# Four small edits at the edges of a two-cache decode attention: a projection moved inside the first tile, the last weight load in four pieces, a later x load, two loads issued ahead of the block

## The chip, the cores and the metric

The kernel runs on one core of a Trainium2 chip. The metric is the device time of one execution in microseconds (us). Beside it each run lists the *span*, the time from the first to the last instruction of the core; here the time is 1.7 us longer than the span in most runs, and that difference becomes a finding further down.

## The reference, cut to what matters

Two independent attention layers, "cache A" and "cache B", each decode one token for 8 batch entries and 32 heads. Every operand is bf16.

```python
B, Sq, D = 8, 1, 1024
H, Sk, Dh = 32, 4096, 128
q = (x @ wq).reshape(B, Sq, H, Dh).transpose(0, 2, 1, 3)
scores = einsum("bhqd,bhkd->bhqk", q, k_cache) * (Dh ** -0.5)
o = einsum("bhqk,bhkd->bhqd", softmax(scores), v_cache)
out = o.transpose(0, 2, 1, 3).reshape(B, Sq, H * Dh) @ wo
# the same for A and for B; the two outputs are concatenated
```

Each cache has 268 MB of k and as much of v, all read once. That makes some 1.1 GB for little arithmetic.

## The kernel before

The work is cut into 64 tiles (2 caches, 8 batch entries, 4 groups of 8 heads). A tile has one k load and one v load of 8.4 MB each, 64 KB per partition. Three ring slots hold them. Each engine runs its own list of operations in order: PE the matrix products, DVE the vector work, ACT copies and the exponential, and SP issues loads. A load is issued by SP when the slot's last user on PE is done.

The order of loads, and the rule by which a load may be issued:

```python
plan = [("wq", 0, 1), ("k", 0, 0), ("wq", 1, 2)]          # (what, which, ring slot)
for n in range(NQ - 1):
    plan.append(("k", n + 1, (n + 1) % 2))
    plan.append(("v", n, 2))
plan += [("v", NQ - 1, NQ % 2), ("wo", 0, 2), ("wo", 1, (NQ - 1) % 2)]
tenant = [None, None, ("x", 0)]
# ... load_tiles(): the next load of the plan depends on opUse of the slot's former tenant:
#     wq -> the q products; k -> the last chunk's sums on PE; v -> the second half of the P.V products
```

So slot 2 has, in turn, x, wq of B, v of tile 0, v of tile 1, and so on. The v load of tile 1 has to wait for the P·V products of tile 0, and those run in chunks 2 and 3 of tile 1.

A tile's k is handled in four chunks (`NR` is 4). DVE multiplies a chunk by q, folds it once, PE sums further, DVE reduces. With cuts:

```python
for n in range(NQ):
    for r in range(NR):
        s = n * NR + r
        make_mul(s)                     # DVE, L330, 4.4 us; waits for k
        if s >= LAG: make_red(s - LAG)  # DVE, L353
        # ... softmax shift and exp of tile n - 1 at r == 0
        fold = make_fold(s)             # DVE, L335, 2.3 us
        # ... make_pm(n - 1) at r == 0: the weights for P.V of tile n - 1
        if n == 0 and r == 1:
            for c in range(1, NC):
                make_q(c)               # PE: x @ wq of B, waits for wq of B; ACT copies the result
                make_qT(c)              # PE transposes, DVE copies four times (L305)
        if r == 2 and n >= 1: make_pv(n - 1, 0, RG // 2)
        if r == 3 and n >= 1: make_pv(n - 1, RG // 2, RG); make_acc(n - 1)
        # ...
        make_eacc(s, fold)              # PE, L345
        load_tiles()
```

The last weight load, wo of B, is cut by heads so that the products can follow the pieces:

```python
wo_cuts = ((0, H - 8), (H - 8, H - 2), (H - 2, H))       # 24, 6 and 2 heads
# ... in load_tiles: one dma per cut, each with its own semaphore ("w", i)
# ... in make_proj, for the last cache:
for i, (r0, r1) in enumerate(wo_cuts):
    def emit(e, r0=r0, r1=r1):
        for r in range(r0, r1):
            for q in range(nt):                           # nt is 4: four products per head
                x = e.matmul(proj[32 * q:32 * q + B, 0:dt], on_sb[:, c, r, :], w[:, col:col + dt], ...)
    opProj[c] = add("pe", emit, [opNorm[c], opT[("wo", c, i)], c_proj, opEv.get(c - 1)])
```

Two more parts that the change touches: x is loaded through ACT's queue with no dependency, and everything, the first loads too, is issued inside one `nc.Block()`.

Of the kernel before, what the change touches and what calls it, by code (L numbers as in the profile page):

```python
# [31 lines left out]
class _Program:  # L32
# [11 lines left out]
    def add(self, eng, emit, deps=(), dma_key=None, moves=False):  # L44
        op = _Op(eng, emit, list(deps), dma_key, moves)
        if dma_key is not None:
            self.counts[dma_key] = self.counts.get(dma_key, 0) + 16
            op.token = (dma_key, self.counts[dma_key])
        for d in op.deps:
            if not (d.eng == "pe" and eng == "pe"):  # L50
                d.sig = True
        self.ops[eng].append(op)
        return op
# [29 lines left out]
            waited.update(left)  # L83
        return out, known

    def run(self, engname, eng, sems, loop=None):
        ops = self.ops[engname]
        waits, known = self._waits(engname)

        def emit(op, at=lambda base, step: base):  # L90
            ins = op.emit(eng, at) if op.moves else op.emit(eng)
            if op.dma_key is not None:
                ins.then_inc(sems[op.dma_key], 16)
            elif op.sig:
                ins.then_inc(sems[op.eng], 1)

        def straight(lo, hi):
            for op, left in zip(ops[lo:hi], waits[lo:hi]):
                for key, val in left.items():
                    eng.wait_ge(sems[key], val)  # L100
                emit(op)

        if loop is None:
            straight(0, len(ops))
            return
        first, per, rounds = loop
        at = [self.marks[first + per * i][engname] for i in range(rounds + 1)]
        size = at[1] - at[0]
        assert all(y - x == size for x, y in zip(at, at[1:]))
        body, step = [], {}  # L110
        for j in range(size):
            rows = [waits[lo + j] for lo in at[:-1]]
            row = {}
            for key in rows[1]:
                grow = rows[2][key] - rows[1][key]
                row[key] = rows[1][key] - grow
                assert step.setdefault(key, grow) == grow

                assert rows[0].get(key) == row[key] or key not in rows[0] and row[key] <= known[at[0] + j].get(key, 0), (engname, j, key)
            for i, r in enumerate(rows):  # L120
                assert ops[at[i] + j].sig == ops[at[0] + j].sig
                assert set(r) <= set(row) and (i == 0 or r == {key: val + i * step[key] for key, val in row.items()}), (engname, j, i)
            body.append(row)
        straight(0, at[0])
        with eng.Fori(0, rounds) as i:
            grown = {x: eng.snap(i * x) for x in sorted(set(step.values()))}
            moved = {}

            def place(base, x):
                if x not in moved:  # L130
                    moved[x] = eng.snap(i * (x * per))
                return moved[x] + base
            for j in range(size):
                for key, val in body[j].items():
                    eng.wait_ge(sems[key], grown[step[key]] + val)  # L135
                emit(ops[at[0] + j], place)
        straight(at[-1], len(ops))


def _build_kernel(nc, caches, out):  # L140
    B, Sq, D = caches[0][0].shape
    _, H, Sk, Dh = caches[0][1].shape
    NC = len(caches)
# [7 lines left out]
    NR = T // CT  # L151
# [8 lines left out]

    es = ExitStack()
    with es:
        block = es.enter_context(nc.Block())
        sb = lambda name, shape, dt: es.enter_context(nc.sbuf_tensor(name, shape, dt))
        ps = lambda name, n=512: es.enter_context(nc.psum_tensor(name, [128, n], FP32))

# [29 lines left out]
        q_ps = [o_ps, pv_ps]  # L196
        misc_bf16 = misc.bitcast(BF16)

        wo_cuts = ((0, H - 8), (H - 8, H - 2), (H - 2, H))
        sems = {e: es.enter_context(nc.semaphore(f"c_{e}")) for e in ENGINES[1:]}  # L200
        for name, n in (("t", 3), ("w", len(wo_cuts)), ("x", 1), ("out", 1)):
            for i in range(n):
# [2 lines left out]
        P = _Program()  # L205
        add = P.add

        def dma(out_ap, in_ap, key, deps, eng="sp"):
            return add(eng, lambda e: e.dma_start(out_ap, in_ap), deps, dma_key=key)
# [16 lines left out]
        c_oh = add("dve", lambda e: e.tensor_copy(own_h[:], own), [c_own])  # L226
# [100 lines left out]
        def make_mul(s):  # L327
            n = s // NR
            v = chunk(s).rearrange("p (t d) -> p t d", d=Dh)
            opMul[s] = add("dve", lambda e: e.tensor_tensor(  # L330
                v, v, qbc[:, n % 2, :].unsqueeze(1).to_broadcast([128, CT, Dh]), ALU.mult), [opT[("k", n)], opQbc[n]])

        def make_fold(s):
            v = chunk(s).rearrange("p (t d) -> p t d", d=Dh)
            return add("dve", lambda e: e.tensor_tensor(v[:, :, 0:64], v[:, :, 0:64], v[:, :, 64:128], ALU.add), [opMul[s]])  # L335
# [15 lines left out]
        def make_red(s):  # L351
            n, r = divmod(s, NR)
            opRed[s] = add("dve", lambda e: e.tensor_reduce(  # L353
                s_sb[:, n % 2, r * CT:(r + 1) * CT], red_ps[s % 2][:, :].rearrange("p (t w) -> p t w", w=16), AX.X, ALU.add),
                [opEacc[s], _at(opExp, n - 2)])


        def make_shift(n):
            m = add("dve", lambda e: e.tensor_reduce(rmax[:], s_sb[:, n % 2, :], AX.X, ALU.max), [opRed[NR * n + NR - 1]])  # L359
            t = add("dve", lambda e: e.tensor_scalar(rtmp[:].rearrange("p (i w) -> p i w", i=2),  # L360
                                                     half[:].unsqueeze(2).to_broadcast([128, 2, 16]), rmax[:, 0:1], scale,
                                                     ALU.add, ALU.mult), [m, c_half])
            opNgm[n] = add("dve", lambda e: e.tensor_reduce(ngm[:, n % 2:n % 2 + 1], rtmp[:], AX.X, ALU.max, negate=True,  # L363
                                                            apply_transpose=True), [t, _at(opExp, n - 2)])
            opExp[n] = add("act", lambda e, at: e.activation(pe[:], s_sb[:, n % 2, :], ACTF.Exp, bias=ngm[:, n % 2:n % 2 + 1], scale=scale,  # L365
                                                             accum_out=rsum[:, bass.ds(at(n, 1), 1)]),
                           [opNgm[n], _at(opPM, n - 1)], moves=True)

        def make_pm(n):
            opPM[n] = add("dve", lambda e: e.tensor_tensor(PM[:], pe[:].unsqueeze(2).to_broadcast([128, T, HQ]),  # L370
                                                           own_h[:].unsqueeze(1).to_broadcast([128, T, HQ]), ALU.mult),
                          [opExp[n], c_oh, _at(opPV, n - 1), opQT["last"] if n == 0 else None])
# [16 lines left out]
        def make_acc(n):  # L389
            opAcc[n] = add("act", lambda e: e.activation(accS[:], pv_ps[:], ACTF.Copy), [opPV[n], _at(opExt, n - 1)])  # L390
# [51 lines left out]


        x_sb = ring[0:B, 2, 0:NC * D].rearrange("p (c d) -> p c d", c=NC)
        op_x = [dma(x_sb[:, c, :], caches[c][0].rearrange("b s d -> b (s d)"), ("x", 0), [], "act") for c in range(NC)]

        def emit_xT(e):
            for c in range(NC):
# [14 lines left out]
        for n in range(NQ):  # L463
            P.mark(n)
            for r in range(NR):
                s = n * NR + r
                make_mul(s)
                if s >= LAG:
                    make_red(s - LAG)
                if r == LAG - 1 and n >= 1:  # L470
                    make_shift(n - 1)
                fold = make_fold(s)
                if r == LAG - 1 and n >= 1:
                    make_pm(n - 1)
                if n == 0 and r == 1:
                    for c in range(1, NC):
                        make_q(c)
                        make_qT(c)
                if r == 2 and n >= 1:
                    make_pv(n - 1, 0, RG // 2)  # L480
                if r == 3 and n >= 1:
                    make_pv(n - 1, RG // 2, RG)
                    make_acc(n - 1)
                if r == 2 and n + 1 < NQ:
                    make_stage(n + 1)
                    make_qbc(n + 1)
                make_eacc(s, fold)
                load_tiles()
                if r == 3 and n >= 1:
                    make_ext(n - 1)  # L490
        P.mark(NQ)
        n = NQ - 1
# [15 lines left out]
            o.token = (("x", 0), 16 * NC)  # L508
        loops = {"pe": (1, 2, (NQ - 2) // 2), "dve": (3, 2, (NQ - 4) // 2), "act": (3, HB, (NQ - 4) // HB)}

        @block.sync
        def _(eng):
            P.run("sp", eng, sems)
            eng.wait_ge(sems[("out", 0)], counts[("out", 0)])

        @block.tensor
# [49 lines left out]
```

## Time and profile before

| | before |
|---|---|
| time, median of 5 runs (range) | 2566.68 us (2566.35 to 2567.43) |
| span of the profiled run | 2565.3 us |
| bytes moved, mean rate | 1107.51 MB, 432 GB/s |
| DVE busy, PE busy | 85%, 44% |

The first view is the profile page. In the line of the tenths, each digit is one of 40 equal slices of the span, and 9 is 90% or more.

```profile
DVE  2898898898898898898888888988988988988983
...
DMA  9999999999999999999999999999999999999998
...
DMA packets 19435, 1107.51 MB, mean 432 GB/s; under 512 B 2209, under 2 KB 2257, under 8 KB 2401
...
q1 hardware_dynamic: 19344, 1107.32, 99.8%
```

The loads fill 99.8% of the time of all 16 DMA engines. No other engine can be the limit, and no edit that leaves the bytes alone can do more than fill the few gaps. To find them one has to look finer than a slice of 64 us. The next view is the timeline of DVE in before, from the start of the multiplies; the columns are start, duration, engine, line, operation, output<-input, and in brackets how long the engine had been idle and what released it.

```profile
55.39 2.28 DVE L335 TENSOR_TENSOR ring<-ring 128x4096 bf16<-128x4096 bf16 x1
69.66 0.43 DVE L305 COPY qT<-misc 128x64 bf16<-128x64 bf16 x1 [11.99 <-PE misc L301]
...
72.67 4.54 DVE L330 TENSOR_TENSOR ring<-ring,qbc 128x8192 bf16<-128x8192 bf16 x1
...
88.12 4.42 DVE L330 TENSOR_TENSOR ring<-ring,qbc 128x8192 bf16<-128x8192 bf16 x1
```

In the middle of tile 0, after chunk 1, DVE stands still for 12 us because the copies of q of cache B come next in its list. The k of tile 0 lies there ready. The last line is chunk 0 of tile 1: it starts at 88.12. The same delay shows on the queue that issues the loads (timeline of SP in before):

```profile
67.90 0.33 SPq L209 DMA_DIRECT2D ring<-in_A_v_cache_dram  x1
91.89 0.33 SPq L209 DMA_DIRECT2D ring<-in_A_k_cache_dram  x1
118.20 0.33 SPq L209 DMA_DIRECT2D ring<-in_A_v_cache_dram  x1
125.70 0.33 SPq L209 DMA_DIRECT2D ring<-in_A_k_cache_dram  x1
```

The third line is the v load of tile 1. The packet records of the trace (start, duration and size of each DMA packet) show what it runs into. The load ahead of it, k of tile 2, ends like this on the 16 engines, and the next load starts like this:

```
before, 64 KB packets near 119 us
ends of the old load:   118.50 118.55 118.55 118.57 118.69 118.71 118.74 118.80 118.80 118.80 118.81 118.83 118.92 118.92 120.14 120.24
starts of the new load: 119.16 119.17 119.17 119.18 119.18 119.26 119.27 119.28 119.30 119.34 119.36 119.36 119.45 119.68 120.24 121.84
duration of the new load's first 14 packets: 2.70 to 3.64 us;  of a packet in the stream: 2.42 us
```

About 1 us passes from the issue to the first packet, the old load is out by then, and the first packets after a pause are slower. The means of the two rows differ by 0.6 us. That is the one hole in the whole record, after the start and before the end, in which the 16 engines stood idle for more than 0.3 us on average.

The last part is the end. The chain that ended last, in before, from the last products of the softmax on (start, duration, what):

```profile
2521.87 34.98 DMA ring<-in_B_wo_dram
2556.84 0.14 issue
2556.98 5.66 PE proj L433 x96
2562.64 0.02 issue
2562.66 0.42 DVE orow L438
```

And the table of stretches for the same kernel; the columns after the stretch are its length, the busy time of PE, PEld, DVE, ACT and POOL with the number of instructions, the granted TensorE clock (1.00 is full), the DMA share and GB/s:

```profile
2557.00:2559.00 2.00, 2.00 (x40) 1.36 (x44) 0.00 (x0) 0.00 (x0) 0.00 (x0) 0.50 0.79 326
2559.00:2561.00 2.00, 2.00 (x47) 1.28 (x39) 0.00 (x0) 0.00 (x0) 0.00 (x0) 0.50 0.22 88
2561.00:2563.00 2.00, 1.61 (x56) 1.15 (x48) 0.34 (x1) 0.00 (x0) 0.00 (x0) 0.99 0.03 10
```

PE starts when the piece of 24 heads has landed, and works without a pause for 5.66 us, most of it at half clock, while the loads thin out and end at 2561.30.

### The profile page before, as it was taken

Reading aid. Unit: us, or ns where it says so; the run is one execution under the profiler, and the core shown is the slowest. Engines: PE = TensorE matmul, PEld = TensorE weight load, DVE = VectorE, ACT = ScalarE, POOL = GpSimd, SP = SyncE. Lnnn points to the kernel's source line nnn. Section 1 sums busy time; section 2 is a strip of 40 time slices with the busy share of each in tenths; the row PEclk is TensorE's granted clock in tenths of the full one; section 3 lists DMA queues with packets and bytes.
Section 4 is the critical chain, followed back from the end, with each engine's and each line's share of the span. In section 5 each row is a group of like instructions: output and inputs, shape, how many; then the busy total and the mean of one; then the engine's idle time right before and its main releaser. Section 6 shows DMA issues by size and latency. Waiting matters only on the chain.

```text
span 2565.3 us, 18707 instructions
## 1 busy us (share of the span) xinstructions
PE 1125.5 (44%) x7648; PEld 395.3 (15%) x7648; DVE 2172.4 (85%) x1043; ACT 130.0 (5%) x401; POOL 2.6 (0%) x14
## 2 busy tenths in 40 slices
PE   2543443444444444444444434444444434434435
PEld 0111111111111111111111111111111111111112
DVE  2898898898898898898888888988988988988983
ACT  1100000000000000000000000000000000000000
POOL 0000000000000000000000000000000000000000
PEclk7666667676766767767766767667766757667677
DMA  9999999999999999999999999999999999999998
GB/s 425 425 425 441 433 433 433 433 435 431 435 431 435 431 435 432 435 431 435 432 435 431 435 431 436 430 436 430 437 429 437 429 437 430 436 431 435 431 436 381
DMA packets 19435, 1107.51 MB, mean 432 GB/s; under 512 B 2209, under 2 KB 2257, under 8 KB 2401
## 3 DMA queue, kind: packets, MB, share of 16 engines
q1 hardware_dynamic: 19344, 1107.32, 99.8%
q8 instruction: 7, 0.11, 0.0%
q10 hardware_dynamic: 80, 0.05, 0.0%
q14 instruction: 4, 0.02, 0.0%
HBM read 1107.33 MB, written 0.03 MB: 432 GB/s over the span
## 4 chain that ended last, share of the span: by engine, by line
DMA 51%; DVE 28%; issue 16%; PE 5%; another core or an unknown queue 0%; ACT 0%; DVEq 0%; SPq 0%
DMA ring<-in_B_k_cache_dram 25%; DMA ring<-in_A_k_cache_dram 25%; DVE ring L330 10%; DVE ring L335 10%; PE red L345 4%; DVE s_sb L353 4%; DVE PM L370 3%; DMA ring<-in_B_wo_dram 1%; DVE rmax L359 1%; DVE rtmp L360 0%; PE proj L433 0%; ACT PM L291 0%; PE o L285 0%; DVEq L135 0%
## 5 line engine op out<-in xcount | busy, mean ns | idle before, releaser
L345 PE MATMUL red<-ring,ident 128*128 128x512 bf16 x2048 | 785.6, 553 | 1380.5 <-DVE ring L335 1380.5
L330 DVE TENSOR_TENSOR ring<-ring,qbc 128x8192 bf16<-128x8192 bf16 x256 | 1131.1, 4418 | 303.4 <-DMA ring<-in_B_k_cache_dram 153.3
L335 DVE TENSOR_TENSOR ring<-ring 128x4096 bf16<-128x4096 bf16 x256 | 581.4, 2271 | 0.0
L345 PEld LDWEIGHTS red<-ring,ident 128*128 128x128 bf16 x2048 | 239.7, 128 | 1833.6 <-DVE ring L335 1482.9
L353 DVE TENSOR_REDUCE s_sb<-red 128x64 f32<-128x1024 f32 x256 | 311.0, 1215 | 3.7 <-PE red L345 3.7
L382 PE MATMUL pv<-ring,PM 128*32 128x512 bf16 x4096 | 274.0, 415 | 4.6 <-DVE PM L370 4.6
L370 DVE TENSOR_TENSOR PM<-pe,own_h 128x2048 bf16<-128x2048 bf16 x64 | 146.1, 2283 | 0.7 <-ACT pe L365 0.7
L382 PEld LDWEIGHTS pv<-ring,PM 128*32 128x32 bf16 x4096 | 103.9, 104 | 189.0 <-issue 116.3
L319 ACT ACTIVATE qbc<-misc 128x128 bf16<-128x128 f32 x64 | 17.8, 278 | 1072.4 <-PE misc L317 1072.4
L365 ACT ACTIVATE pe<-s_sb,ngm 128x256 bf16<-128x256 f32 x64 | 32.5, 508 | 468.5 <-DVE ngm L363 468.5
L390 ACT ACTIVATE accS<-pv 128x512 bf16<-128x512 f32 x64 | 38.2, 597 | 349.0 <-PE pv L382 349.0
L399 PEld LDWEIGHTS o<-accS,E 128*32 128x32 bf16 x1024 | 31.3, 100 | 49.4 <-issue 48.2
L399 PE MATMUL o<-accS,E 128*32 128x32 bf16 x1024 | 38.1, 185 | 0.7 <-ACT accS L390 0.7
L405 ACT ACTIVATE o_sb<-o 32x32 f32 (+1 forms) x64 | 11.9, 186 | 454.4 <-PE o L399 453.8
L305 DVE COPY qT<-misc 128x64 bf16<-128x64 bf16 x8 | 3.5, 435 | 33.3 <-PE misc L301 33.3
L359 DVE TENSOR_REDUCE rmax<-s_sb 128x1 f32<-128x256 f32 x64 | 26.9, 420 | 2.2
L438 DVE CAST orow<-proj 40x512 bf16<-40x512 f32 (+1 forms) x2 | 1.1, 554 | 26.7 <-PE proj L433 26.7
L433 PE MATMUL proj<-ring,on_sb 128*8 128x256 bf16 (+1 forms) x192 | 15.2, 395 | 13.8 <-DMA ring<-in_A_wo_dram 8.7
L312 ACT ACTIVATE qst<-qT 128x128 bf16 (+1 forms) x64 | 18.7, 293 | 2.0 <-DVE qT L305 2.0
L360 DVE TENSOR_SCALAR rtmp<-half,rmax 128x32 f32<-128x32 f32 x64 | 15.4, 241 | 2.2
L285 PE MATMUL o<-ring,xT 128*8 128x512 bf16 x64 | 7.1, 621 | 20.0 <-DMA ring<-in_A_wq_dram 11.0
L363 DVE TRANSPOSE_TENSOR_REDUCE ngm<-rtmp 128x1 f32<-128x32 f32 x64 | 13.5, 211 | 2.2
(33 smaller groups left out, 74.4 us busy)
## 6 DMA issues: line engine op xcount, KB each, us to landing
ring<-in_B_wo_dram SPq DMA_DIRECT2D x1, 6144.0 KB, 35.0
ring<-in_B_wo_dram SPq DMA_DIRECT2D x1, 1536.0 KB, 38.3
ring<-in_A_k_cache_dram SPq DMA_DIRECT2D x32, 40.0
ring<-in_A_v_cache_dram SPq DMA_DIRECT2D x32, 27.9
ring<-in_B_k_cache_dram SPq DMA_DIRECT2D x32, 39.8
ring<-in_B_v_cache_dram SPq DMA_DIRECT2D x32, 27.9
ring<-in_B_wo_dram SPq DMA_DIRECT2D x1, 512.0 KB, 39.0
out_dram<-orow SPq DMA_DIRECT2D x2, 4.0 KB
```

What stands on the lines that cost most here:

```text
L312: return e.activation(qst[:, n % 2, :].rearrange("p (j m) -> p j m", m=MP), from_.unsqueeze(2).to_broadcast([128, HQ, MP]), ACTF.Copy)
L319: opQbc[n] = add("act", lambda e: e.activation(qbc[:, n % 2, :], misc[:, 0:Dh], ACTF.Copy), [opQb[n], _at(opMul, NR * (n - 2) + NR - 1)])
L330: opMul[s] = add("dve", lambda e: e.tensor_tensor(v, v, qbc[:, n % 2, :].unsqueeze(1).to_broadcast([128, CT, Dh]), ALU.mult), [opT[("k", n ...
L335: return add("dve", lambda e: e.tensor_tensor(v[:, :, 0:64], v[:, :, 0:64], v[:, :, 64:128], ALU.add), [opMul[s]])
L345: i = e.matmul(dst, ident[:], v[:, g, :, j, :], start=(j == 0), stop=(j == 3))
L353: opRed[s] = add("dve", lambda e: e.tensor_reduce(s_sb[:, n % 2, r * CT:(r + 1) * CT], red_ps[s % 2][:, :].rearrange("p (t w) -> p t w", w ...
L359: m = add("dve", lambda e: e.tensor_reduce(rmax[:], s_sb[:, n % 2, :], AX.X, ALU.max), [opRed[NR * n + NR - 1]])
L365: opExp[n] = add("act", lambda e, at: e.activation(pe[:], s_sb[:, n % 2, :], ACTF.Exp, bias=ngm[:, n % 2:n % 2 + 1], scale=scale, accum_ou ...
L370: opPM[n] = add("dve", lambda e: e.tensor_tensor(PM[:], pe[:].unsqueeze(2).to_broadcast([128, T, HQ]), own_h[:].unsqueeze(1).to_broadcast( ...
L382: i = e.matmul(pv_ps[32 * q:32 * (q + 1), :], PM[:, t:t + 4, :].rearrange("p t j -> p (t j)"), v[:, t * Dh:(t + 4) * Dh], start=(g == 0), ...
L390: opAcc[n] = add("act", lambda e: e.activation(accS[:], pv_ps[:], ACTF.Copy), [opPV[n], _at(opExt, n - 1)])
L399: x = e.matmul(to, E[:, i, PH - 1 - u:PH - 1 - u + MB], accS[:, i * 128 + H * u:i * 128 + H * (u + 1)], start=(i == 0 and u == 0), stop=(i ...
```

## The change

The intent is to win the last idle moments of the DMA engines: close the wait in tile 0, let the last projection follow its load more closely, and start the first load earlier. The diff, with the plumbing of a `part` argument cut:

```diff
-    def run(self, engname, eng, sems, loop=None):
+    def run(self, engname, eng, sems, loop=None, part=(0, None)):
...
-        wo_cuts = ((0, H - 8), (H - 8, H - 2), (H - 2, H))
+        wo_cuts = ((0, 12), (12, 24), (24, H - 2), (H - 2, H))
...
-        op_x = [dma(x_sb[:, c, :], caches[c][0]..., ("x", 0), [], "act") for c in range(NC)]
+        op_x = [dma(x_sb[:, c, :], caches[c][0]..., ("x", 0), [c_oh], "act") for c in range(NC)]
...
-                if n == 0 and r == 1:
+                if n == 0 and r == NR - 1:
                     for c in range(1, NC):
                         make_q(c)
                         make_qT(c)
...
-        block = es.enter_context(nc.Block())          # was ahead of all allocations
...
+        P.run("sp", nc.sync, sems, part=(0, 2))       # the first two loads
+        block = es.enter_context(nc.Block())
         @block.sync
         def _(eng):
-            P.run("sp", eng, sems)
+            P.run("sp", eng, sems, part=(2, None))
```

`c_oh` is a small constant that DVE makes at the start (done at 2.46 us in before).

More of the change, by code (lines that the diff above doesn't have):

```diff
@@ L103, in run @@
         if loop is None:
-            straight(0, len(ops))
+            straight(part[0], len(ops) if part[1] is None else part[1])
             return
@@ L444, in _build_kernel @@
         x_sb = ring[0:B, 2, 0:NC * D].rearrange("p (c d) -> p c d", c=NC)
-        op_x = [dma(x_sb[:, c, :], caches[c][0].rearrange("b s d -> b (s d)"), ("x", 0), [], "act") for c in range(NC)]
+        op_x = [dma(x_sb[:, c, :], caches[c][0].rearrange("b s d -> b (s d)"), ("x", 0), [c_oh], "act") for c in range(NC)]
         def emit_xT(e):
```

## The prediction

> **What bounds the kernel.** The loads. The page's DMA line has 1107.5 MB at a mean 432 GB/s, their queue at 99.8% of the 16 engines' time; DVE has 85%, PE 44%. The rate is next to the 435 GB/s that the Trainium skill ("DMA: Bandwidth & Descriptors", "Where 436 GB/s comes from") gives as the ceiling of the path into SBUF; this trace agrees with 432. The bytes do not change, so only time in which a DMA engine has nothing queued can be won.
>
> **Where such time is, in before.**
> 1. Start. The wq load is issued at 0.81 us, 0.07 us after the barrier released SP (chain of waits), x on ACT at 0.80. In the packet records the x packets run at 1.77 us; the first 64 KB packets begin between 1.86 and 2.66, mean near 2.1.
> 2. One hole. The v load of tile 1 is issued at 118.20 us (timeline); it waits for the P·V products of tile 0. The k load ahead of it runs dry at 118.5 to 118.9 on most engines, the next packets start at 119.2 to 119.5: some 0.5 us of 16 idle engines, and the first packets after it take about 3.1 us instead of 2.42. No other hole of that size is in the records. The cause: DVE sat from 57.7 to 72.9, in the middle of tile 0, behind q of cache B, whose wq landed near 62.6.
> 3. End. The last packets end at 2561.3; but PE started the first 24 heads of the last projection when that piece landed (2556.84 in the chain) and ran without a wait, at half clock until 2561 (table of stretches), to 2562.63: behind the loads.
>
> **What the change does.**
> - q of B moves to chunk 3 of tile 0. DVE multiplies and folds chunks 2 and 3 (4.4 + 2.3 us each) in the time it used to wait. By the durations in the trace tile 1 starts when its k lands, near 81.5 us rather than 88.2; the v load of tile 1 is issued near 111.5, and the hole closes. The v load of tile 0 is issued near 75 instead of 67.9, still 5 us before the k load ahead of it ends. Estimated gain: 0.5 + 0.7 = 1.2 us.
> - First two loads outside the block: one branch less, 0.07 us. x behind a DVE constant (done at 2.46): x no longer goes first, the 64 KB packets should start near 1.75 on all engines. Together about 0.3 us. x lands perhaps at 12 to 14 us instead of 10.7; it is needed at 22.8, no cost.
> - wo in 12, 12, 6, 2: 12 heads land near 2549.6 and run right after the first projection's cast (2552.6). PE then catches up, waits for the last piece, and has 8 products left: end near 2561.9 to 2562.0 instead of 2562.63, gain about 0.7 us. One more issue on SP (0.43 us), hidden.
>
> The sum is 2.2 us, below 0.1%.
>
> **Predicted: 2564.5 us, 8 in 10 between 2562.5 and 2566.5.** Faster by over 2%: 0.005; within 2%: 0.99; slower: 0.005.
>
> **What would show it.** Right: no packet gap near 119 us, v of tile 1 issued near 111; first 64 KB packets near 1.75; PE waiting for a wo piece between 2558 and 2562, the chain ending through the DMA of the 2-head piece. Wrong: a new gap near 80 us; the last projection unbroken to its end.
>
> **What could make it wrong.** The end is set by the slowest of 16 engines, and their drift (2558.0 to 2561.3 at the end) is as large as the gain; another chip may differ by more.

## The result, and the profile after

| | before | after |
|---|---|---|
| time, median of 5 runs | 2566.68 us | 2565.28 us |
| range | 2566.35 to 2567.43 | 2564.61 to 2566.12 |
| span of the profiled run | 2565.3 us | 2563.2 us |
| spans of the 5 runs | not listed | 2562.7 to 2563.2 us |

The ratio is 0.9994, with a 95% interval of 0.9982 to 1.0007. It is computed as the mean time of the changed kernel's fast runs over the mean of the other's fast runs of the same rounds, so it is not quite the ratio of the medians. The interval is wider than the effect, but the two sets of five times do not overlap, and neither do those of a repeat (below). The measured gain is 1.4 us by the medians, where 2.2 was predicted; the span of the profiled run shrank by 2.1.

The timeline of DVE after, the same stretch:

```profile
55.85 2.28 DVE L334 TENSOR_TENSOR ring<-ring 128x4096 bf16<-128x4096 bf16 x1
58.05 4.42 DVE L329 TENSOR_TENSOR ring<-ring,qbc 128x8192 bf16<-128x8192 bf16 x1
...
74.48 0.43 DVE L304 COPY qT<-misc 128x64 bf16<-128x64 bf16 x1 [1.00 <-PE misc L300]
...
82.58 4.43 DVE L329 TENSOR_TENSOR ring<-ring,qbc 128x8192 bf16<-128x8192 bf16 x1 [4.77 <-DMA ring<-in_A_k_cache_dram]
```

The wait of 12 us has become 1 us, and tile 1 starts at 82.58, as soon as its k has landed; DVE now even waits 4.77 us for it. The queue of SP after:

```profile
72.72 0.33 SPq L208 DMA_DIRECT2D ring<-in_A_v_cache_dram  x1
80.89 0.33 SPq L208 DMA_DIRECT2D ring<-in_A_k_cache_dram  x1
112.67 0.33 SPq L208 DMA_DIRECT2D ring<-in_A_v_cache_dram  x1
120.09 0.33 SPq L208 DMA_DIRECT2D ring<-in_A_k_cache_dram  x1
```

The v load of tile 1 is issued 5.5 us earlier, and in the packet records all engines pass from one load to the next at 118.7 to 120.7 us without a gap, with packets of 2.42 us. The start of the chain of waits after still has the first load where it was (0.81 in before, too):

```profile
0.74 0.07 issue
0.81 0.41 SPq L208
```

The end of the chain after, and its table of stretches:

```profile
2520.42 38.15 DMA ring<-in_B_wo_dram
2558.57 0.04 issue
2558.61 1.91 PE proj L432 x18
2560.52 0.02 issue
2560.54 0.42 DVE orow L437
```

```profile
2557.00:2559.00 2.00, 1.24 (x26) 0.52 (x22) 0.00 (x0) 0.00 (x0) 0.00 (x0) 0.50 0.58 235
2559.00:2561.00 2.00, 1.49 (x28) 0.54 (x20) 0.42 (x1) 0.00 (x0) 0.00 (x0) 0.50 0.01 5
```

The timeline of PE shows the same stretch piece by piece:

```profile
2555.12 2.73 PE L432 MATMUL proj<-ring,on_sb 128*8 128x256 bf16 x48 [4.14 <-DMA ring<-in_B_wo_dram]
2558.61 1.88 PE L432 MATMUL proj<-ring,on_sb 128*8 128x256 bf16 x32 [0.76 <-DMA ring<-in_B_wo_dram]
```

PE does stop and wait now, but for the second piece (4.14 us) and for the piece of 6 heads (0.76 us), not for the last one. The 32 products of the last 8 heads follow in one run of 1.9 us, all of it at half clock: the clock records show the fall to 0.50 at 2553.5, in the first of these two waits. The last packet ended at 2559.32, the last product at about 2560.5.

One more thing came out of comparing times with spans. Time minus span is 1.72 us in most runs, but in the five runs of the changed kernel it was 1.71, 2.08, 2.38, 2.63 and 2.92. In the packet records, the last packet of the instruction queue (q8, 16 KB, the program text that an engine fetches) stands at 2561.65 in before, inside the span. In the changed kernel's profiled run it starts at 2565.44, after the span has ended at 2563.19, and ends at 2566.43; that run's time was 2566.12.

### The profile page after: what moved, and what is told of

It reads as the page before. It is cut to its first block, busy times and chain, and to the rows that moved or that the text cites. A ratio compares the mean times of both kernels' runs of the same rounds, so it can differ in the third digit from the quotient of the medians.

```text
span 2563.2 us, 18707 instructions
## 1 busy us (share of the span) xinstructions
PE 1122.2 (44%) x7648; PEld 395.1 (15%) x7648; DVE 2173.1 (85%) x1043; ACT 130.0 (5%) x401; POOL 2.6 (0%) x14
## 3 DMA queue, kind: packets, MB, share of 16 engines
q1 hardware_dynamic: 19488, 1107.32, 99.9%
## 4 chain that ended last, share of the span: by engine, by line
DMA 52%; DVE 28%; issue 16%; PE 4%; another core or an unknown queue 0%; ACT 0%; DVEq 0%; SPq 0%
DMA ring<-in_A_k_cache_dram 25%; DMA ring<-in_B_k_cache_dram 25%; DVE ring L329 10%; DVE ring L334 10%; PE red L344 4%; DVE s_sb L352 4%; DVE PM L369 3%; DMA ring<-in_B_wo_dram 1%; DVE rmax L358 1%; DVE rtmp L359 0%; ACT PM L290 0%; DVEq L135 0%; DVE ngm L362 0%; PE proj L432 0%
## 5 line engine op out<-in xcount | busy, mean ns | idle before, releaser
L316 PE MATMUL misc<-ident,qst 128*128 128x128 bf16 x64 | 14.8, 232 | 0.9 <-ACT qst L311 0.9
```

## The experiments

Twelve kernels ran, in three batches of four; each batch has nine runs of the kernel before on the same chip. The theory (H): closing the hole near 119 us is what shortens the span; the start gives nothing; the tail gives little, and loses part of it again outside the span. The rivals: (P) the gain is divided as the prediction has it; (D) the gain is the drift of the slowest DMA engine from run to run.

In the table, "idle" is the mean over the 16 engines of the time without a packet of any queue between 110 and 130 us (counted from the packet records: 16 less the packets under way, summed over time, divided by 16), and "tail" the time from the end of the last wo packet to the end of the last product; both are from the profiled run of each.

| run | time, mean of 5 | time of before, mean of 9 | span, mean of 5 | time minus span | v of tile 1 issued | idle | tail |
|---|---|---|---|---|---|---|---|
| ctl_before | 2566.58 | 2566.72 | 2564.86 | 1.69 to 1.75 | 117.91 | 0.18 | 1.68 |
| q_only | 2565.09 | 2566.72 | 2563.36 | 1.69 to 1.77 | 112.30 | none | 2.07 |
| wo_only | 2567.32 | 2566.72 | 2565.30 | 1.71 to 2.71 | 118.72 | 1.10 | 1.12 |
| block_only | 2566.98 | 2566.72 | 2565.26 | 1.69 to 1.77 | 118.35 | 0.41 | 1.21 |
| no_q | 2566.39 | 2566.72 | 2564.30 | 1.72 to 3.05 | 118.65 | 0.77 | 0.86 |
| before_d9 | 2572.36 | 2566.72 | 2570.60 | 1.73 to 1.82 | 124.47 | 6.20 | 0.86 |
| after_d22 | 2570.58 | 2566.72 | 2568.78 | 1.71 to 1.92 | 122.25 | 4.20 | 1.13 |
| warm | 2564.52 | 2566.72 | 2562.76 | 1.69 to 1.83 | 112.34 | none | 0.92 |
| after_again | 2565.27 | 2567.18 | 2562.94 | 1.71 to 2.83 | 112.24 | none | 1.13 |
| lean | 2564.37 | 2567.18 | 2562.62 | 1.70 to 1.81 | 112.51 | none | 0.86 |
| pe_pad | 2564.74 | 2567.18 | 2563.02 | 1.69 to 1.80 | 112.06 | none | 1.12 |
| dve_pad | 2564.80 | 2567.18 | 2562.84 | 1.69 to 2.61 | 112.13 | none | 1.13 |

The nine runs of before had a mean span of 2564.97, 2564.99 and 2565.43 us in the three batches. For the first profile pair the idle is 0.59 and none, the tail 1.30 and 1.16.

### ctl_before: the kernel before, sent again

No edit.

> Control: the kernel before, sent again, timed against itself. Theory H (the hole near 119 us is a property of the program): a ratio of 1.000, spans within 0.5 us of 2565.3, and the same hole in the packet records, 16 engines idle some 0.5 us between 118.5 and 120. Rival D (what was gained is the drift of the slowest engine from run to run): spans that differ by 1 us and more among themselves, with some as low as the 2562.7 to 2563.2 of the changed kernel.

The ratio is 1.0 (0.9986 to 1.0014). The hole is there again, smaller, as the v load came 0.3 us sooner. The spans of the control's five runs go from 2564.2 to 2566.0. So the kernel before has a drift of about 2 us from run to run, which is as large as the effect, and part of what rival D says is true of it. But not one of its runs, here or in the three sets of nine (2563.9 to 2566.5), comes down to 2563.3, and none of the ten spans of the changed kernel is above that. The expectation of spans within 0.5 us was too tight.

### q_only: only the move of q

```diff
-                if n == 0 and r == 1:
+                if n == 0 and r == NR - 1:
```

> Only q of cache B moved to the last chunk of tile 0. Theory H: this part alone closes the hole; v of tile 1 issued near 112.7 us instead of 118.2, no engine idle near 119, span shorter by 1.0 to 2.0 us (2563.3 to 2564.3), so nearly all of the gain of the whole change. Theory as recorded in the prediction: 1.2 us of 2.2. Rival D: no difference from the control beyond its own spread.

The hole is gone, and the mean span is 1.6 us shorter than the nine runs of before beside it (2563.36 against 2564.97), the mean time as well (2565.09 against 2566.72). One line of the change has the whole gain in time that the changed kernel had in its first measurement. None of its five spans (2562.9 to 2563.8) overlaps with those of the nine runs of before (2564.0 to 2566.1), so drift alone does not explain it. The tail is at its longest here, 2.07 us: the loads end earlier, and PE, with 24 heads in one piece at half clock, does not.

### wo_only: only the four pieces

```diff
-        wo_cuts = ((0, H - 8), (H - 8, H - 2), (H - 2, H))
+        wo_cuts = ((0, 12), (12, 24), (24, H - 2), (H - 2, H))
```

> Only the last wo in four pieces. Prediction: PE ends 0.7 us earlier against the last packet, so the span is shorter by 0.7 us. Theory H with what the changed kernel's trace shows (PE still runs unbroken, at half clock, over the last 32 products): the time from the end of the last packet to the end of the last product stays 1.2 us against 1.33, so the span is shorter by 0.1 to 0.2 us at most. The hole near 119 us stays.

No gain: the mean span is 0.3 us longer and the mean time 0.6 us longer than that of before. The span alone settles nothing at this size, because the hole happened to be large in the profiled run (1.10 us) and drifts. What counts is the difference between time and span: up to 2.71 us, where every kernel with three pieces stays below 1.9. The late instruction packet is here too, at 2566.47, 1.8 us after the end of the span.

### block_only: only the first two loads outside the block

The diff is the last part of the change above.

> Only the first two loads outside the block. Prediction: wq issued 0.07 us earlier, at 0.74. What the changed kernel's trace shows: issued at 0.81 in both, so 0.0 us in the span. Open: the times of the changed kernel were shorter by 1.4 us but its span by 2.1 to 2.6; if starting loads outside the block adds time outside the span, this run has time minus span about 1 us larger than the control.

The wq load is issued at 0.80 us, as in the control. The span is 2565.26 against 2564.97 on average, so there is no gain. Time minus span stays at 1.72, so the block is not what added time outside the span.

### no_q: everything but the move of q

```diff
-                if n == 0 and r == NR - 1:
+                if n == 0 and r == 1:
```

(against the changed kernel)

> The changed kernel with q of cache B put back to chunk 1; the other three parts stay. Theory H (the closed hole is the whole gain of the span): v of tile 1 is issued near 118.4 us again, the idle engines near 119 come back, span mean near the control's 2564.9 and no gain in time; the time may even be above the control's, since four pieces of wo added 0.3 to 0.6 us outside the span so far. Rival P (the prediction's sizes): 1.0 us of gain stays, span near 2563.9.

The hole is back at 118.65 us. The mean span is 0.7 us shorter than that of before, and the mean time 0.3 us. That is more than H expected and less than P. Half of the 0.7 is lost again outside the span (1.72 to 3.05). In this profile PE happened to be at full clock for the last pieces (tail 0.86), unlike in wo_only, which has the same wo loads. With holes that differ by 0.3 us between two profiles, these two kernels show only roughly what the other parts give without the move of q: between a loss of 0.6 us in time (`wo_only`, the pieces alone) and a gain of 0.3 (`no_q`, all three).

### before_d9: the suspected delay, larger

```diff
                         make_q(c)
                         make_qT(c)
+                    for _ in range(9):
+                        c_proj = add("dve", lambda e: e.memset(proj[:], 0.0), [c_proj])
```

> The kernel before with nine idle clears of PSUM (0.48 us each, some 4.4 to 4.9 us in all) on DVE in tile 0 right behind q of cache B. Result unchanged. Theory H: v of tile 1 comes that much later, the hole near 119 us grows from 0.2-0.5 us to about 5 us, and the time grows by as much, 4.4 to 4.9 us, to about 2571.3. Rival D (run-to-run drift, DVE not on the path of the loads): unchanged within 0.5 us.

The result is right and the time is 5.6 us longer, 2572.36 against 2566.72. Each clear takes 0.48 us, but the next starts only 0.67 us after it, since it waits for it by semaphore; so the delay was 6.0 us, not 4.4 to 4.9. The v load of tile 1 moved from 118.2 to 124.47, the idle time grew from about 0.6 to 6.20 us, and these 5.6 us show at the end. DVE is not the bottleneck of the kernel as a whole, and yet its work in tile 0 costs nearly its full length, because in this one place it decides when a load may start. Rival D falls in the form in which it was put for this run, that DVE is not on the path of the loads; that the gain itself is more than drift rests on the spans of `q_only` and of the changed kernel, which do not overlap with those of before.

### after_d22: a delay that uses up the reserve

The same edit on the changed kernel, at its new place, with 22 clears.

> The changed kernel with 22 such clears (some 11 us) on DVE at the same place. Theory H: DVE has 4.8 us of idle before tile 1 and v of tile 1 a reserve of about 5 us, so of 11 us about 10 are hidden: v of tile 1 is issued near 119, the hole comes back at about 0.5 to 1.5 us with the slow first packets behind it, and the span returns to 2564.5 to 2566. A rival that has DVE work of tile 0 on the critical path would give 11 us, another that has it never there gives 0.

22 clears at 0.67 us are 14.7 us, so the expectation's 11 us were wrong in the same way. Of the 14.7 us, DVE's wait for k (4.77 in after) hid about 5 and the v load of tile 1 came 9.6 us later (122.25 against 112.67). Of these 9.6, the reserve hid 5.4, and 4.20 us of idle engines came out; with the slow packets behind the pause (some 0.7 us, as in the other holes) that makes 4.9, and the mean span grew by 5.9 (2568.78 against 2562.88). The remaining 1 us is not accounted for by the mean over the engines. The span of 2564.5 to 2566 that was expected was missed by 3 us and more, since the delay was longer than reckoned. Both extremes fall: the delay is neither fully on the path nor fully off it, and the reserve of 5.4 us is what the move of q had bought.

### warm: PE kept at full clock in the tail

```diff
                 opProj[c] = add("pe", emit, [opNorm[c], opT[("wo", c, i)], c_proj, opEv.get(c - 1)])
+                if c == NC - 1 and i < 2:
+                    def keep(e, k=(15, 7)[i]):
+                        for _ in range(k):
+                            x = e.matmul(red_ps[0][:, 0:512], ident[:], accS[:], start=True, stop=True)
+                        return x
+                    add("pe", keep, [opRed[NS - 1], opAcc[NQ - 1]])
```

> The changed kernel with 15 and 7 products without use (128x512, into a free PSUM bank) on PE while it waits for the second and the third piece of wo. Theory: PE is then at full clock for the last 32 products, which take about 1.0 us instead of 1.88 once data is there; the last product ends 0.8 us after the last packet instead of 1.2, span shorter by about 0.35 us (2562.5). Beside that, the 16 KB packet of instructions that in kernels with four pieces came after the end of the span (2565.4) and in kernels with three before it: if it hangs on the place of PE in its program, 44 more instructions bring it back into the span, and time minus span falls from a mean of 2.3 to 1.7.

The timeline of PE in this run, from the first half of the last projection on; the lines with `red` are the products without use:

```profile
2555.74 1.48 PE L432 MATMUL proj<-ring,on_sb 128*8 128x256 bf16 x48
2557.38 1.46 PE L439 MATMUL red<-accS,ident 128*128 128x512 bf16 x6 [0.16 <-issue]
2558.77 0.83 PE L432 MATMUL proj<-ring,on_sb 128*8 128x256 bf16 x24
2559.86 0.39 PE L432 MATMUL proj<-ring,on_sb 128*8 128x256 bf16 x8 [0.27 <-DMA ring<-in_B_wo_dram]
```

The piece of 6 heads now takes 0.83 us, PE waits for the last piece, and 8 products of 0.39 us are left, which is just the picture that the prediction had drawn for the change itself. The tail is 0.92 us, against 1.16 in the changed kernel and 1.13 in its repeat, and the mean span falls to 2562.76. The 0.35 us expected in the span came out as 0.1 to 0.2. The larger gain is outside: the instruction packet stands at 2557.16, inside the span, and time minus span is 1.69 to 1.83 in all five runs.

### after_again: the changed kernel, as a control

No edit.

> The changed kernel again, as a control for the other three of this batch. Span mean near 2562.9, time minus span scattered from 1.7 to 2.9 with a mean above 2.0, and the last 16 KB instruction packet of the profiled run after the end of the span.

The five times (2564.77 to 2565.84) lie below all nine of before beside them (2566.42 to 2567.63). Time minus span is scattered again: 1.71, 1.87, 2.54, 2.70, 2.83. One part of the expectation failed, and usefully: in this profiled run the instruction packet was inside the span, at 2559.66, and that run's time minus span was 1.72. So the same kernel has it early in some executions and late in others, and the time follows.

### lean: without the two parts that did nothing

The kernel before with the move of q, the four pieces and the products of `warm`; x and the block as before.

> The kernel before with only q of cache B in chunk 3, wo in four pieces, and the products that keep PE at full clock; x as before, the first two loads inside the block as before. Theory H (x and the block did nothing): span and time as those of the run with all four parts and the same products, 2562.8 and 2564.5, within 0.3 us. Prediction as recorded: 0.3 us longer, since it gave x and the block 0.3 us.

The means are 2562.62 in the span and 2564.37 in time, against 2562.76 and 2564.52 for `warm`. Taking the x dependency and the block away cost nothing; the two kernels ran on different chips, but beside its own runs of before `lean` gained more (2.8 us against 2.2 in the span). It was the fastest of all kernels here, at 0.9989 of before (0.9975 to 1.0002), that is 2.8 us by the means.

### pe_pad and dve_pad: whose program the late packet belongs to

```diff
+        def pad(e):                                   # pe_pad, ahead of make_proj(0), PE idle there
+            for _ in range(6):
+                x = e.matmul(red_ps[0][:, 0:512], ident[:], accS[:], start=True, stop=True)
+            return x
+        add("pe", pad, [opRed[NS - 1], opAcc[NQ - 1]])
```

> The changed kernel with six products without use on PE while it waits for the first wo, 2533 to 2540 us; 12 more instructions on PE, the loads untouched. If the late instruction packet hangs on where PE's program ends, it moves to before the end of the span and time minus span goes to 1.7 to 1.8 in all runs; the span stays 2562.9. If it hangs on DVE's program: time minus span stays scattered with a mean above 2.0.

```diff
         make_qbc(0)
+        for _ in range(12):                           # dve_pad, DVE idle there
+            c_proj = add("dve", lambda e: e.memset(proj[:], 0.0), [c_proj])
```

> The changed kernel with twelve clears of PSUM on DVE in its idle time before the first multiply, 34 to 43 us (8.0 us at 0.67 us each); PE's program untouched. If the late instruction packet hangs on the place of PE in its program: as the changed kernel, time minus span scattered with a mean above 2.0. If on DVE's (the run with 22 clears had none of it): 1.7 to 1.8 in all runs. Span near 2562.9 either way.

Twelve more PE instructions leave the span at 2563.02 and bring time minus span to 1.69 to 1.80 in all five runs; the packet stands at 2557.07. Twelve clears on DVE leave it scattered (1.69, 1.74, 1.79, 1.98, 2.61), and the packet stands at 2564.68, after the end. That points to PE's program. In `pe_pad`, `warm` and `lean`, the kernels with more PE instructions, the packet starts at 2557.07 to 2557.39, ahead of the 2559.66 of the early case of `after_again`, and none of their 15 runs has a time minus span above 1.83, where 7 of the 10 runs of the changed kernel have 2.08 or more. But clears on DVE did not leave all as it was: `dve_pad` has 2 of 5 runs above 1.9 and a mean of 1.96, just under the 2.0 that was expected if DVE has no part. With five runs each it is not shown that PE alone decides. The four profiled runs with the late packet agree on the rest:

| run | end of the span | end of the late packet | time | time minus end of the packet |
|---|---|---|---|---|
| after | 2563.19 | 2566.43 | 2566.12 | -0.31 |
| wo_only | 2564.71 | 2567.71 | 2567.41 | -0.30 |
| no_q | 2564.41 | 2567.75 | 2567.45 | -0.30 |
| dve_pad | 2563.01 | 2565.91 | 2565.61 | -0.30 |

In the nine profiled runs of the three batches in which it was early, the time is the span plus 1.72 or 1.73 us. These are coincidences in time; that the late fetch itself makes the execution longer, and not something that delays both, is likely but not shown. An odd one is left: `after_d22` has four pieces and PE's program unchanged, and was early in its profile and near 1.7 to 1.9 in all runs. Why it was spared is open, as is what in a given execution decides between early and late.

## Why the prediction was right or wrong

The range and the class held, and the sum of 2.2 us came out as 1.4 to 1.9 (medians of the first measurement, means of the repeat). That the range held says little: it is 4 us wide and ends 0.2 us below the median of before, so a gain of 0.2 us would have been enough. And that the sum came so near is partly luck, for the term of the hole was too small, that of the start and (by the mean tails) that of the end too large, and a loss outside the span was not foreseen. Term by term:

- **What bounds the kernel: right.** The loads keep their 99.8% (99.9% after), and everything that was won was idle time of the DMA engines or time behind the last packet.
- **The hole: right in mechanism and place, a little more in size.** "the v load of tile 1 is issued near 111.5, and the hole closes": it is issued at 112.67, and there is no gap. The term of 1.2 us came out as 1.6 us in `q_only`. Following the packets of the engines end to start gives the reason. The mean of the 16 engines' last packets moved from 2559.3 (five kernels with the hole: both of before, wo_only, block_only, no_q) to 2558.1 (seven without it), that is 1.2 us as predicted. The slowest engine moved by 1.6, from 2560.9 to 2559.3 on average: without the hole the engines also end closer together. `before_d9` and `after_d22` show the mechanism in both directions.
- **The v load of tile 0: right.** It was put near 75 us and came at 72.72, with no new gap near 80.
- **The start: wrong.** "the 64 KB packets should start near 1.75 on all engines. Together about 0.3 us." The load is issued at 0.81 us in both traces (with one branch less ahead of it), and the first 64 KB packets start at 1.84 to 2.68 us, mean 2.05 against 2.10. They then take 3.15 us on average instead of 2.97 (3.06 in the control), so the second packets start at the same time as before (4.85 to 5.39). The x packets had not held anything up. `block_only` and `lean` agree: 0.0 us. x was used at 15.97 us, later than the 12 to 14 predicted, and still at no cost, since wq landed at about 23.
- **The end: the term was mis-sized.** "PE then catches up, waits for the last piece, and has 8 products left … gain about 0.7 us". It caught up with the second piece and fell behind again with the third. The Trainium skill says in "TensorE: Matmul & The Clock Gate" (Part 1: The HAM clock gate) that PE falls to half clock when idle and is released after some 3.4 us of work. The traces agree in the main: in before the clock was released 4.1 us after PE had started (2556.98 to 2561.04); after the change it was at 0.50 over all of the last 32 products, which took 1.88 us, with a wait of 0.76 us just before them. `warm` shows 0.83 + 0.39 us for them at full clock. The prediction had read the half clock in before and did not carry it over to a PE that would now wait more. It also reckoned from the end of the last packet without the 0.5 us or so that pass before PE may start (2559.28 to 2559.75 in `lean`). The chain accordingly goes through the DMA of the 6-head piece, not of the 2-head piece as announced. The tail came down from 1.4 us (mean of five profiles with three pieces) to 1.1 (mean of seven with four pieces and no products in the tail), 0.3 us instead of 0.7. The tail that the prediction reckoned with, 0.6 to 0.7 us behind the last packet at 2561.3, came out as 1.12 to 1.16 in the four profiles of the changed kernel and its padded forms. But the 0.3 is a mean over kernels with and without the hole. With the hole closed the tail was 2.07 in `q_only` and 1.12 to 1.16 in those four, and the mean span was 2563.36 against 2562.84 to 2563.02; so beside the move of q the other parts, the pieces above all, may be worth 0.3 to 0.5 us of span as the means stand, and 0.8 to 1.0 when `after_again`, `pe_pad`, `dve_pad` and `q_only` are each taken against the runs of before beside them. They ran on different chips, `q_only` has one profile, and the size stays open.
- **What was not in it at all:** with the four pieces the last instruction fetch came after the end of the span in part of the executions. Time minus span is 2.15 us on average over the 25 runs of after, after_again, wo_only, no_q and dve_pad, the kernels with four pieces in which the late packet was seen or whose code is the same, against 1.7, a loss of 0.4 us. (With `after_d22`, which has the same PE program and was spared, it is 2.09.) With it, this part of the change is worth about nothing by the mean tails, and at most some 0.6 us. That sums up as 1.6 + 0.0 + 0.3 - 0.4 = 1.5 us, where the means gave 1.6 in the first measurement and 1.9 in the repeat; the rest may be the end term, which the mean tails may take too small.

The remark about the slowest engine was right to the point that it should have been an argument. The Trainium skill ("DMA: Bandwidth & Descriptors", in "Why a DMA increments its semaphore by 16 and not by 1") says that the up to 16 engines of a load finish independently and the semaphore counts them; the records agree, with last packets at 2558.0 to 2561.3 in before.

## What to carry to other kernels

In a kernel whose loads fill the DMA engines, an engine with 15% of idle time can still own a microsecond: look for the load that is issued less than its start latency (here 1 us) before the queue runs dry, and follow its slot back to the work that freed it. In these runs a pause cost about its length plus a slow first round of packets, and what was added to it on purpose (`before_d9`) came out in the total nearly one for one (5.6 of 6.0 us). When the sizes reach a microsecond, compare the time and the span of each run separately, for an edit may shorten one and lengthen the other, and when work is split to follow the data more closely, ask at what clock it will run after it has waited.

## What the Trainium skill lacked or had wrong

- "DMA: Bandwidth & Descriptors": nothing was found there on the slow restart. The first 64 KB packets of all engines after a pause take about 3.1 us (most of 2.9 to 3.3) against 2.42 us in the stream, and the same at the start of the kernel; a hole therefore cost about 0.7 us beyond its own length.
- The same page gives a fixed cost of about 2.0 us per DMA for the path through GpSimd, most of it the receipt after the last byte, and 0.6 us to the first byte for the path through SP and ACT that is used here. Here it was about 1.0 us from issue to first packet (118.20 to 119.16) and about 0.5 us from the end of the last packet to the engine that waited for it (2559.28 to 2559.75).
- No page found, "Runtime: NRT & Kernel Launch" with its part on instruction fetch included, that says what a fetch of 16 KB at the end of a program does to the device time. In four profiled runs it started after the last instruction, and the time ended 0.30 us before the fetch did, up to 1.3 us later than otherwise. With 12 more instructions on PE the fetch was inside the span in the profile, and time minus span stayed at 1.80 or less in all five runs.
- "TensorE: Matmul & The Clock Gate" was borne out in the main: half clock after waiting, and varying from run to run in when it is released (0.50 in wo_only's last products, full clock in no_q's). It puts the fall to half clock after an idle window of about 3.4 us; here a shorter wait was enough: in `dve_pad` PE waited 2.51 us, until 2554.75, and the clock fell at 2556.01.
